# Low parts of the first expert on VectorE, its inputs in another buffer, and a later planned PE for the routing chain

## The chip, the cores and the metric

The program runs on 1 core of one Trainium2 chip. The metric is device time in microseconds (us) of one execution; lower is better. PE is TensorE, DVE is VectorE, ACT is ScalarE, POOL is GpSimd, SP is SyncE, which here only issues DMAs.

## The reference

Three layers follow one another on 4 sequences of 576 tokens: an attention with 8 heads that keeps only scores within `tau` of each row's maximum, a mixture of 8 experts (512 to 1024 to 512) with one expert per token, and a gated MLP.

```python
scores = scale * np.matmul(q, k.transpose(0, 1, 3, 2))
thresh = np.max(scores, axis=-1, keepdims=True) - tau
scores = np.where(scores >= thresh, scores, -1e9)
x = softmax(scores) @ v                       # then (B, S, 512)
...
logits = x @ w_gate; local_gate = sigmoid(x @ w_local)
for b, s:                                     # routing runs along the tokens
    fresh_e = argmax(logits[b, s])
    e = fresh_e if s == 0 or local_gate[b, s] < 0.5 else prev_e
    prev_e = e
    out[b, s] = softmax(logits[b, s])[e] * (np.maximum(x[b, s] @ w1[e], 0) @ w2[e])
...
h = gelu(x @ w_in); u, v = halves of h
out = x + (u * (w_sg @ layernorm(v) + b_sg)) @ w_out
```

Since a token's expert can be that of the token before, the routing is a chain of small dependent steps.

## The kernel before

**Order.** The kernel first makes a list of operations with their dependences, a guessed duration and a due time (`Op`, `Graph`, `Flow`). `Graph.order` plays a list scheduler over it once, when the program is built, and the instructions are written in the order that it finds. On the chip each engine runs its own queue strictly in that order: an instruction that waits holds up everything behind it on its engine. An operation marked `fill` may be put by the planner into a gap in front of a later one.

**Matmuls in two parts.** Every fp32 operand is used as a rounded high part and a low part (the rest), and a product takes three matmuls: high by high, high by low, low by high. For a weight chunk of 128 x 1024, `split` in `Tail.moe` makes the high part on ACT (`whi`) and the low part on DVE or POOL (`wlo`: raw chunk minus high part). Which engine takes it is written in a string with a letter per chunk, `WLO` for experts two to eight and `WLOA` for the first.

**The stages around the change.** The attention works on 144 tiles, whose softmax steps are on DVE (`mx`, L442, and `mask`, L466), POOL (`nb`, L452) and ACT (`ex`, L457). Each half of the tokens has a routing chain (`Route.half`): some 40 small operations, nearly all on DVE, with transposes and small matmuls on PE (L1063, L1067, L1070, L1077, L1078, and L1134 at the end, which gives the row numbers of the tokens). The first half's chain runs amid the attention. It names the expert with the most tokens, whose weights are loaded early (4 chunks of w1, 4 of w2), and picks two tiles of 128 tokens (`plain`). These two tiles need only the first half, so they are the work that PE has while the second half's chain runs: A1 is their first layer (96 matmuls of 128 x 256 columns, `fill`), A2 the second (48 matmuls of 128 x 512). `first` makes high and low part of A1's result (`hh` on ACT, `hl` on DVE). After the second half's chain POOL gathers three more tiles of the same expert (`xin`), and PE goes on with them at `L1`. `Route.rest` follows on DVE: it orders the other experts and gives the rows of the other tiles.

**Names.** Nearly all operations of the experts show line L193, that of a helper. In rows `c` (c_75 to c_80) are raw weight chunks or the attention's cells, `MR` and `r` the areas that hold rounded parts, `MF` the rest of the memory, `inv` the gathers' row numbers. The memory is cut into cells (`Mem.CELLS`); a cell that the attention has used is taken anew for rounded parts only when all of the attention's work in it is done. `RAW` are the attention's two raw buffers, at 20480 and 22528; `TURN` is the order in which the twelve weight slots are used, a slot being 2048 words at 2048 times its number; slots 0 to 3 lie in `MR`, slots 4 to 9 in the cell at 8192.

Of the kernel before, what the change touches and what calls it, by code (L numbers as in the profile page):

```python
# [8 lines left out]
F32 = mybir.dt.float32  # L9
# [5 lines left out]
AX = mybir.AxisListType  # L15
# [4 lines left out]
T = B * S  # L20
# [2 lines left out]


class Op:
    __slots__ = ("eng", "dur", "deps", "emit", "prio", "start", "end", "n", "name", "need", "cls", "users", "banks", "fill")

    def __init__(self, eng, dur, prio, emit, name):
        self.eng, self.dur, self.prio, self.emit, self.name = eng, dur, prio, emit, name
        self.need, self.cls, self.users, self.banks, self.fill = 0, None, [], None, False  # L30


class Graph:
# [4 lines left out]
        PE=dict(PE=0.0, DVE=0.2, ACT=0.2, POOL=0.27, DQ=1.29),  # L38
        DVE=dict(PE=0.256, DVE=0.12, ACT=0.135, POOL=0.156, DQ=1.22),
        ACT=dict(PE=0.227, DVE=0.145, ACT=0.1, POOL=0.17, DQ=1.245),  # L40
        POOL=dict(PE=0.161, DVE=0.075, ACT=0.12, POOL=0.1, DQ=1.17),
# [18 lines left out]
    def order(self, alpha=1.0, smax=3):  # L60
        ops = self.ops
        users = [[] for _ in ops]
        need = [0] * len(ops)
# [18 lines left out]
        def enter(o):  # L82
            t = 0.0
            for d in o.deps:
                t = max(t, d.end + self.lat(d, o.eng))
            at[o.n] = t
            ready.setdefault(o.eng, []).append(o)

# [11 lines left out]
        for o in ops:  # L100
            if not need[o.n]:
                enter(o)
        left = len(ops)
        while left:
            best = None
            for e, lst in ready.items():
# [9 lines left out]
                if c is not None and cs > f + self.GAP:  # L116
                    b = None
                    for o in lst:
                        if o.fill:
                            s = when(o, f)  # L120
                            if s + o.dur <= cs + self.GAP and (b is None or (s + alpha * o.prio, o.n) < (b[0], b[2].n)):
                                b = (s + alpha * o.prio, s, o)
# [4 lines left out]
            s, e, o = best  # L127
# [3 lines left out]
            if o.need:  # L131

                if o.need == 2:
                    b = max((b for b in (0, 2, 4, 6) if max(bank[b], bank[b + 1]) <= s), key=lambda b: max(bank[b], bank[b + 1]))
# [7 lines left out]
            for h in hold.get(o.n, ()):  # L142
                left_users[h.n] -= 1
                if not left_users[h.n]:
                    t = max(x.end + self.lat(x, "PE") for x in h.users)
# [661 lines left out]
def act(n, ps=False):  # L807
    return (0.05 if ps else 0.093) + n / 1200.0


def dve(n, two=False):
    return 0.069 + n / (1920.0 if two else 960.0)
# [6 lines left out]
def pe(n, k=1):  # L819
    return k * max(n / 2400.0 + 0.014, 0.12)  # L820


class Use:


    __slots__ = ("prev", "w", "r", "i")
# [17 lines left out]
class Bank:  # L844
    __slots__ = ("first", "w", "ap")
# [76 lines left out]
def route_consts(tc, cst):  # L922

    nc = tc.nc
    v = nc.vector
    at = [Route.CONST]

# [61 lines left out]
class Route:  # L989
# [5 lines left out]

    AT, AB, AO, SIZE = Mem.F + 8368, Mem.F + 4424, Mem.F + 5448, 3290
    CONST = AT + SIZE

    def __init__(self, g, tc, cst, prio):
        self.g, self.nc, self.cst, self.prio = g, tc.nc, cst, prio  # L1000
# [29 lines left out]

    def op(self, eng, n, emit, *deps, pr=None, pw=None, w=(), late=0.0):
        dur = n if eng in ("PE", "DQ") else dve(n) if eng == "DVE" else act(n)
        return self.g.op(eng, dur, self.p + late, emit, deps=deps, pr=pr, pw=pw, w=w, name="rt")

    def half(self, h, deps):

# [280 lines left out]
class Tail:  # L1317
# [5 lines left out]
    P = dict(more=-12.300, wld=19.348, whi=-5.770, wlo=11.562, gth=36.897, cv=31.147, xT=12.357, s=25.298, mgth=16.824, sgl=-12.676, fin=9.956, vh=63.991, sg=25.660, wo=50.081)  # L1323
    WLO = "DDDDDDDD"

    WLOA = "DDPPPPDP"
    PH = 4.0

    WR = tuple(33792 + 1024 * i for i in range(6))
    F = Mem.F  # L1330
    TURN = (0, 1, 2, 4, 6, 7, 8, 9, 5, 3, 10, 11)
    XG = (F + 6920, F + 6344, F, F + 512, F + 1024)
    XT, HH, HL, YO, G, IDX = 24576, 27648, 30720, (F + 1736, F + 2248, F + 2888), F + 4936, F + 6856
    AX, AH = 6144, (20480, 22528)
    CVA, CVF, CVC = F + 3400, (F + 8368, F + 8880, F + 9392, F + 9904), F + 10416

    def __init__(self, tc, g, cst, w1, w2, route):
# [12 lines left out]
    def slot(self, n):  # L1350
        s = self.TURN[n]
        return self.M(2048 * s, [128, 1024], F32R), self.M(2048 * s + 1024, [128, 1024], F32R)
# [15 lines left out]
    def moe(self, dep, x_dram, ys, side, sw):  # L1368

        nc, g = self.nc, self.g  # L1370
# [6 lines left out]
            wr=Ring(g, [[(a, 1024)] for a in self.WR]),  # L1377
            wh=Ring(g, [[(2048 * i, 1024)] for i in self.TURN]),
            wl=Ring(g, [[(2048 * i + 1024, 1024)] for i in self.TURN]),
            xg=Ring(g, p512(self.XG)),  # L1380
            yo=Ring(g, p512(self.YO)),
        )
        W = lambda t: self.W0 + self.ALPHA[0] * t
# [84 lines left out]
        def plain(T):  # L1468
# [10 lines left out]
            w = [ld(i, T + 1.7 * i) for i in range(4)]  # L1479
            W8 = [split(*w[i], V(T), self.WLOA[i]) for i in range(4)]  # L1480
            w += [ld(i, T + 5) for i in range(4, 8)]
            W8 += [split(*w[i], V(T + 3 + 1.3 * (i - 4)), self.WLOA[i]) for i in range(4, 8)]
            hh, hl = (self.M(a, [128, 8, z], F32R) for a in self.AH)
            hu = [g.use(*[(a + z * m, z) for a in self.AH]) for m in range(8)]
            for m in range(8):
                p = Bank()
                s = slice(m * 128, (m + 1) * 128)
                for c in range(4):
# [7 lines left out]
                    T += pe(z, 3)  # L1496
                first(m, p, hh, hl, z, hu[m], V(T) - self.PH, V(T) - self.PH)
            for t in range(NA):
# [11 lines left out]
        T, W8 = plain(0.0)  # L1510
        switch(*Mem.CELLS[3])
        base, free = NA, []
        for k, cap in enumerate(CAPS):
# [4 lines left out]
            pitch = 128 * len(tiles)  # L1518
            z = SLOTS[k] - (128 * NA if k == 0 else 0)
# [6 lines left out]
            if k:  # L1526
                st = {}
                W8 = []
                for i in range(8):
                    need = W(T + 0.3 * i if i < 4 else T + L1 + 1.3 * (i - 4))  # L1530
                    W8.append(split(*load(i, k, need, st, [dep["rank"], self.hold0]), need, self.WLO[i]))
            hh, hl = self.M(self.HH, [128, 8, pitch], F32R), self.M(self.HL, [128, 8, pitch], F32R)
            hu = [g.use((self.HH + pitch * m, pitch), (self.HL + pitch * m, pitch)) for m in range(8)]
            if k == 0:

                for x in (hh, hl):
                    g.op("POOL", 0.6, W(T - 10), lambda x=x, a=z, b=pitch: nc.gpsimd.memset(x[:, :, a:b].bitcast(F32), 0.0), w=hu, name="half")
            free = []
            for m in range(8):
                p = Bank()  # L1540
# [14 lines left out]
            for i, t in enumerate(tiles):  # L1555
                c = slice(i * 128, (i + 1) * 128)
                T = second(t, hh[:, :, c], hl[:, :, c], W8, hu, T, [R["last"]] if t == NT - 1 else ())
# [6 lines left out]
        p, o = Bank(), last  # L1564
# [6 lines left out]
        for _ in range(5):  # L1571
            o = g.op("PE", 0.645, W(T + 6), idle, deps=[o], pw=p, name="idle")
# [558 lines left out]
```

## Time and profile before

| | |
|---|---|
| median of 3 runs | 786.31 us (784.88 to 786.63) |
| the profiled execution | 785.32 us, of which the span from the first to the last instruction is 783.5 us |
| granted TensorE clock, mean over the span | 0.995 |
| PE busy | 754.4 us, 96% |
| DVE busy | 590.1 us, 75% |
| ACT busy | 456.6 us, 58% |
| POOL busy | 284.4 us, 36% |

An engine is busy while an instruction of its own runs; the shares are of the span. PE is the busiest, so its idle stretches, and the stretches in which its clock is granted at half, are where the time can change. A row of the timeline ends with the idle time before it and the instruction that ended this.

### The profile page before, as it was taken

Reading aid. Unit: us, or ns where it says so; the run is one execution under the profiler, and the core shown is the slowest. Engines: PE = TensorE matmul, PEld = TensorE weight load, DVE = VectorE, ACT = ScalarE, POOL = GpSimd, SP = SyncE. Lnnn points to the kernel's source line nnn. Section 1 sums busy time; section 2 is a strip of 40 time slices with the busy share of each in tenths; the row PEclk is TensorE's granted clock in tenths of the full one; section 3 lists DMA queues with packets and bytes.
Section 4 is the critical chain, followed back from the end, with each engine's and each line's share of the span. In section 5 each row is a group of like instructions: output and inputs, shape, how many; then the busy total and the mean of one; then the engine's idle time right before and its main releaser. Section 6 shows DMA issues by size and latency. Waiting matters only on the chain.

```text
span 783.5 us, 14050 instructions
## 1 busy us (share of the span) xinstructions
PE 754.4 (96%) x4916; PEld 652.5 (83%) x4916; DVE 590.1 (75%) x1241; ACT 456.6 (58%) x841; POOL 284.4 (36%) x435
## 2 busy tenths in 40 slices
PE   8999999999999896999999999999999999999997
PEld 5787887888787775899898998889788988888996
DVE  7999999999889979575886768794479733677632
ACT  6888888788888583163435436534486522456410
POOL 6434253433443335132533222333483333310420
PEclk9999999999999998999999999999999999999999
DMA  7342324553241441697567586733620022200012
GB/s 217 127 126 61 125 82 134 173 164 126 62 131 55 162 142 63 201 309 257 202 228 244 177 279 234 258 127 135 212 82 0 1 68 85 78 14 0 15 40 68
DMA packets 46911, 103.14 MB, mean 132 GB/s; under 512 B 7540, under 2 KB 7540, under 8 KB 46836
## 3 DMA queue, kind: packets, MB, share of 16 engines
q1 hardware_dynamic: 43636, 91.72, 35.1%
q0 software_dynamic: 3200, 10.49, 4.5%
q8 instruction: 39, 0.64, 0.3%
q14 instruction: 36, 0.29, 0.1%
HBM read 80.17 MB, written 22.02 MB: 130 GB/s over the span
## 4 chain that ended last, share of the span: by engine, by line
PE 76%; DVE 10%; ACT 8%; issue 3%; DMA 1%; POOL 1%; SPq 0%; POOLq 0%; DVEq 0%; ACTq 0%
PE PS L193 51%; PE PS L437 8%; PE PS L525 7%; PE PS L486 5%; ACT MF L457 2%; PE PS L527 2%; PE PS L540 2%; DVE MF L193 2%; DVE r L193 2%; DVE MF L442 2%; ACT c L379 1%; DVE MF L466 1%; ACT MF L193 1%; ACT MR L390 1%; POOL rq L193 1%
## 5 line engine op out<-in xcount | busy, mean ns | idle before, releaser
L193 PE MATMUL PS<-r,r 128*128 128x512 f32 (+5 forms) x1572 | 315.4, 352 | 3.4 <-DVE r L193 3.0
L193 PEld LDWEIGHTS PS<-r,r 128*128 128x128 f32 x1572 | 265.2, 188 | 36.4 <-DVE r L193 4.5
L437 PE MATMUL PS<-MR 128*128 128x288 f32 x640 | 123.4, 322 | 6.5 <-DVE MF L466 4.4
L466 DVE SCALAR_TENSOR_TENSOR MF<-PS,MF 128x576 f32<-128x576 f32 x144 | 116.0, 811 | 7.9 <-ACT MF L457 6.1
L457 ACT ACTIVATE MF<-PS,MF 128x576 f32<-128x576 f32 x144 | 106.7, 751 | 16.1 <-DVE MF L442 9.2
L442 DVE TENSOR_REDUCE MF<-PS 128x1 f32<-128x576 f32 x144 | 106.1, 751 | 4.9 <-PE PS L437 3.6
L193 PE MATMUL PS<-MR,r 128*128 128x256 f32 (+2 forms) x628 | 105.2, 322 | 0.5 <-DVE r L193 0.5
L437 PEld LDWEIGHTS PS<-MR 128*128 128x128 f32 x640 | 93.3, 192 | 14.8 <-DVE MF L466 7.9
L193 PEld LDWEIGHTS PS<-MR,r 128*128 128x128 f32 x628 | 93.8, 190 | 8.7 <-DVE r L193 0.9
L193 ACT ACTIVATE r<-PS 128x512 fp32r<-128x512 f32 (+7 forms) x110 | 47.9, 451 | 86.4 <-PE PS L193 83.8
L379 ACT ACTIVATE c<-PS 128x512 f32<-128x512 f32 (+1 forms) x160 | 85.9, 564 | 17.9 <-PE PS L486 16.8
L486 PE MATMUL PS<-ident,MF 128*128 128x128 f32 x576 | 84.9, 274 | 1.2 <-DVE c L556 0.5
L193 ACT ACTIVATE MF<-PS 128x512 f32<-128x512 f32 (+1 forms) x64 | 35.6, 558 | 79.0 <-PE PS L193 67.8
L452 POOL TENSOR_TENSOR MF<-MF,cf 128x1 f32<-128x1 f32 x120 | 28.3, 237 | 137.8 <-DVE MF L442 124.7
L486 PEld LDWEIGHTS PS<-ident,MF 128*128 128x128 f32 x576 | 67.9, 140 | 4.8 <-ACT c L379 2.1
L193 DVE SCALAR_TENSOR_TENSOR MF<-MF,PS 128x384 f32<-128x384 f32 (+1 forms) x84 | 49.9, 606 | 22.7 <-ACT MF L193 21.9
L193 DVE TENSOR_TENSOR r<-c,r 128x1024 fp32r<-128x1024 f32 x41 | 54.2, 1336 | 15.3 <-ACT r L193 14.7
L193 DVE SCALAR_TENSOR_TENSOR r<-PS,r 128x352 fp32r<-128x352 f32 (+4 forms) x72 | 30.7, 432 | 38.2 <-ACT r L193 37.8
L193 POOL TENSOR_SCALAR MF<-MF 128x512 f32<-128x512 int32 x12 | 20.5, 1704 | 95.1 <-DVE MF L193 58.1
L193 ACT ACTIVATE r<-c 128x1024 fp32r<-128x1024 f32 x47 | 48.4, 1054 | 5.9 <-PE PS L193 4.6
L193 PE MATMUL PS<-r,MR 128*128 128x352 f32 (+3 forms) x288 | 46.0, 295 | 1.7 <-DVE r L193 1.3
L193 ACT ACTIVATE r<-MF 128x256 fp32r<-128x256 f32 (+1 forms) x48 | 15.7, 358 | 53.7 <-DVE MF L193 53.5
(241 smaller groups left out, 1066.6 us busy)
## 6 DMA issues: line engine op xcount, KB each, us to landing
c<-in_w_dram SPq DMA_DIRECT2D x64, 512.0 KB, 5.3
c<-in_kP_dram SPq DMA_DIRECT2D x32, 288.0 KB, 2.9
c<-in_qP_dram SPq DMA_DIRECT2D x32, 288.0 KB, 3.0
ys<-MF SPq DMA_DIRECT2D x36, 256.0 KB, 3.9
x_dram<-c SPq DMA_DIRECT2D x6, 768.0 KB, 4.4
MF<-in_w_in_dram SPq DMA_DIRECT2D x8, 512.0 KB, 4.8
c<-in_vP_dram SPq DMA_DIRECT2D x12, 320.0 KB, 4.9
out_dram<-MF SPq DMA_DIRECT2D x12, 256.0 KB, 2.0
```

The costliest lines, as they stand in the source:

```text
L193: return lambda *a, **k: x(*[v(y) for y in a], **{n: v(y) for n, y in k.items()})
L379: self.nc.scalar.activation(out, src, AF.Copy, **k)
L390: self.nc.scalar.activation(out, src, AF.Copy, scale=f)
L437: self.nc.tensor.matmul(self.PS[:, banks[hf], 0:288], q, k[:, 288 * hf:288 * hf + 288], start=(n == 0), stop=(n == len(ops) - 1))
L442: self.nc.vector.tensor_reduce(m, self.tl[i]["s"], axis=AX.XY, op=ALU.min)
L452: (self.nc.vector if eng == "DVE" else self.nc.gpsimd).tensor_tensor(self.nbt(i), self.tl[i]["m"], self.tp, op=ALU.add)
L457: self.nc.scalar.activation(e.rearrange("p (a b) -> p a b", a=2), t["s"], AF.Exp, bias=t["m"], scale=-1.0)
L466: self.nc.vector.scalar_tensor_tensor(w.rearrange("p (a b) -> p a b", a=2), t["s"], self.nbt(i), t["e"].rearrange("p (a b) -> p a b", a=2) ...
L486: self.nc.tensor.transpose(p[:, c, :], t["w"][:, z + c * 128:z + (c + 1) * 128], self.cst["ident"])
L525: self.nc.tensor.matmul(av[r], v, self.wt(j, b)[:, c, cols], start=(c == 0), stop=False)
L527: self.nc.tensor.matmul(av, self.v4(P)[:, b, :], self.wr(P)[:, x0:x0 + 288], start=False, stop=True)
L540: self.nc.tensor.matmul(r[:, c, :], self.x2T()[:, t * 128:(t + 1) * 128], self.R[:, P % (H // 2), :])
```

## The change

- `WLOA`: the first expert's eight low parts are all made on DVE. Before, chunks 3, 4, 5, 6 and 8 of them were made on POOL.
- `AX`, `AH` and `TURN`: the two tiles' input parts stand in the attention's first raw buffer (20480) and no longer in weight slot 3 (6144). The high part of A1's result is in the second raw buffer, its low part in slot 5. The first expert's first four chunks now take slots 0 to 3, all in `MR`; the fourth was in slot 4 before.
- `PH`: the due time of `hh` and `hl` is no longer put 4 units ahead.
- `PZ`: the two POOL fills that clear the padding of the three tiles' results have a due time 60 units after L1 and no longer 10 ahead of it.
- `LAG`: for the routing chain's steps on PE the planner takes the operands to be there 0.3 us later than by its own costs.

```diff
 class Op:
-    __slots__ = (..., "users", "banks", "fill")
+    __slots__ = (..., "users", "banks", "fill", "lag")
...
     def __init__(self, eng, dur, prio, emit, name):
...
-        self.need, self.cls, self.users, self.banks, self.fill = 0, None, [], None, False
+        self.need, self.cls, self.users, self.banks, self.fill, self.lag = 0, None, [], None, False, 0.0
...
         def enter(o):
             t = 0.0
             for d in o.deps:
-                t = max(t, d.end + self.lat(d, o.eng))
+                t = max(t, d.end + self.lat(d, o.eng) + o.lag)
...
 class Route:
+    LAG = 0.3
...
     def op(self, eng, n, emit, *deps, pr=None, pw=None, w=(), late=0.0):
-        return self.g.op(eng, dur, self.p + late, emit, deps=deps, pr=pr, pw=pw, w=w, name="rt")
+        o = self.g.op(eng, dur, self.p + late, emit, deps=deps, pr=pr, pw=pw, w=w, name="rt")
+        o.lag = self.LAG if eng == "PE" else 0.0
+        return o
...
 class Tail:
-    WLOA = "DDPPPPDP"
-    PH = 4.0
+    WLOA = "DDDDDDDD"
+    PH = 0.0
+    PZ = 60
...
-    TURN = (0, 1, 2, 4, 6, 7, 8, 9, 5, 3, 10, 11)
+    TURN = (0, 1, 2, 3, 6, 7, 8, 9, 4, 5, 10, 11)
...
-    AX, AH = 6144, (20480, 22528)
+    AX, AH = 20480, (22528, 10240)
...
                 for x in (hh, hl):
-                    g.op("POOL", 0.6, W(T - 10), lambda x=x, a=z, b=pitch: nc.gpsimd.memset(x[:, :, a:b].bitcast(F32), 0.0), w=hu, name="half")
+                    g.op("POOL", 0.6, W(T + self.PZ), lambda x=x, a=z, b=pitch: nc.gpsimd.memset(x[:, :, a:b].bitcast(F32), 0.0), w=hu, name="half")
```

Line numbers of the changed kernel are 3 higher in `Route.half` (L1063 is L1066 there).

On DVE, between the end of the attention and the start of the second half's chain, before. L556 scales the attention's last results, L573 sums the logits, L1052 to L1059 are the chain's first steps, and `MR<-PS` are the low parts of the two tiles' inputs:

```order
L573 TENSOR_REDUCE MF<-c_80 128x27
L193 TENSOR_TENSOR MR<-PS,MR 128x4x128 x2
L556 TENSOR_TENSOR c_74<-PS,MF 128x3x128
L556 TENSOR_TENSOR c_80<-PS,MF 128x3x18
L573 TENSOR_REDUCE MF<-c_80 128x27
L1052 SCALAR_TENSOR_TENSOR MF<-MF 128x9
```

The same place now:

```order
L573 TENSOR_REDUCE MF<-c_80 128x27
L193 TENSOR_TENSOR r_2737<-PS,r_2737 128x4x128 x2
L193 TENSOR_TENSOR MR<-c_77,MR 128x1024
L193 TENSOR_TENSOR MR<-c_78,MR 128x1024
L193 TENSOR_TENSOR r_3112<-c_79,r_3112 128x1024
L556 TENSOR_TENSOR c_74<-PS,MF 128x3x128
L556 TENSOR_TENSOR c_80<-PS,MF 128x3x18
L193 TENSOR_TENSOR r_3112<-c_75,r_3112 128x1024
L573 TENSOR_REDUCE MF<-c_80 128x27
L1055 SCALAR_TENSOR_TENSOR MF<-MF 128x9
```

Two low parts (c_77, c_78) stand ahead of the last L556, a third (c_79) there too, and a fourth (c_75) ahead of the last L573. Of the other two that are left, one (c_76) follows behind the chain's step L1062, where before the low part from c_75 stood, and the last (c_80) stands between L1084 and L1085, where before none did. Between L1069 and L1074 four `hl` stand where there were two.

On PE, from the attention's last matmul (L527) to the chain's third step, before. The 128x256 rows are A1:

```order
L527 MATMUL PS<-c_74,c_73 128x288
L193 MATMUL PS<-MR 128x256 x6
L540 MATMUL PS<-MF 128x146 x3
L193 MATMUL PS<-MR 128x256 x21
L1063 MATMUL PS<-ident,MF 9x128
L193 MATMUL PS<-MR,r_3111 128x256 x9
L193 MATMUL PS<-MR 128x256 x3
L1067 MATMUL PS<-ident,MF 9x9
L193 MATMUL PS<-MR 128x256 x6
L1070 MATMUL PS<-ident,MF 128x9
```

The same place now:

```order
L527 MATMUL PS<-c_74,c_73 128x288
L193 MATMUL PS<-r_2737,MR 128x256 x6
L540 MATMUL PS<-MF 128x146 x3
L193 MATMUL PS<-r_2737,MR 128x256 x48
L1066 MATMUL PS<-ident,MF 9x128
L193 MATMUL PS<-r_2737,MR 128x256 x12
L1070 MATMUL PS<-ident,MF 9x9
L193 MATMUL PS<-r_2737,MR 128x256 x9
L1073 MATMUL PS<-ident,MF 128x9
```

54 of the 96 matmuls of A1 now stand ahead of the chain's first transpose, where 27 did. Further on, all 96 of A1 and 3 of A2 stand ahead of the first 18 matmuls that give the three tiles' rows (L1134), and 9 of A2 ahead of the second 18; before, 60 and 72 of A1 and none of A2 did.

On POOL, from the attention's last step (L548) to the three tiles' gathers, before:

```order
L548 TENSOR_SCALAR MF<-MF 128x6
L193 TENSOR_TENSOR MR<-c_77,MR 128x1024
L193 TENSOR_TENSOR r_3111<-c_78,r_3111 128x1024
L193 TENSOR_TENSOR r_3111<-c_79,r_3111 128x1024
L193 TENSOR_TENSOR r_3111<-c_76,r_3111 128x1024
L193 TENSOR_TENSOR r_3111<-c_80,r_3111 128x1024
L193 MEMSET r_3178 128x8x112 x2
L193 DMA MF<-x_dram,inv_91 128x512 x3
```

And now:

```order
L548 TENSOR_SCALAR MF<-MF 128x6
L193 MEMSET r_3193 128x8x112 x2
L193 DMA MF<-x_dram,inv_91 128x512 x3
```

The five low parts are gone. The two fills have stayed ahead of the three gathers.

## Rows read from the trace of the kernel before

**Rows 1.** The page's busy line: time, share of the span, instructions.

```profile
PE 754.4 (96%) x4916; PEld 652.5 (83%) x4916; DVE 590.1 (75%) x1241; ACT 456.6 (58%) x841; POOL 284.4 (36%) x435
```

**Rows 2.** Windows: PE, PEld, DVE, ACT, POOL busy, PE clock, DMA share, GB/s.

```profile
291.60:311.00 19.40, 11.74 (x111) 10.75 (x109) 17.97 (x48) 8.41 (x18) 11.56 (x7) 0.91 0.21 68
340.00:500.00 160.00, 159.54 (x921) 143.22 (x920) 116.95 (x176) 77.38 (x117) 53.18 (x39) 1.00 0.70 237
312.00:314.00 2.00, 2.00 (x11) 2.00 (x10) 1.86 (x10) 0.18 (x1) 1.50 (x2) 0.50 0.30 90
```

**Rows 3.** Timeline of PE: start, us, instructions, idle before and releaser.

```profile
291.59 2.77 PE L193 MATMUL PS<-MR 128*128 128x256 f32 x21
...
297.48 0.38 PE L1063 MATMUL PS<-ident,MF 128*9 128x128 f32 x1 [3.12 <-DVE MF L1059]
297.52 2.27 PE L193 MATMUL PS<-MR,r 128*128 128x256 f32 x9
...
300.88 0.17 PE L1067 MATMUL PS<-ident,MF 9*9 9x9 f32 x1 [0.45 <-DVE MF L1066]
...
310.40 0.61 PE L1134 MATMUL PS<-MF 128*128 128x3 bf16 x18 [4.09 <-ACT MF L1116]
310.88 2.27 PE L193 MATMUL PS<-MR 128*128 128x256 f32 x9
...
326.81 3.00 PE L193 MATMUL PS<-r,r 128*128 128x512 f32 x12
329.65 1.29 PE L193 MATMUL PS<-r,MR 128*128 128x272 f32 x9
```

**Rows 4.** Timeline of DVE, the chain's stretch, and one step of the first half's.

```profile
244.81 0.16 DVE L1054 TENSOR_TENSOR MF<-MF 128x9 f32<-128x9 f32 x1
...
291.96 0.68 DVE L556 TENSOR_TENSOR c<-PS,MF 128x384 f32<-128x384 f32 x2 [2.83 <-PE PS L540]
...
293.29 0.96 DVE L1052 SCALAR_TENSOR_TENSOR MF<-MF 128x9 f32<-128x9 f32 x1
...
294.31 2.24 DVE L1054 TENSOR_TENSOR MF<-MF 128x9 f32<-128x9 f32 x1
...
297.34 1.22 DVE L193 TENSOR_TENSOR r<-c,r 128x1024 fp32r<-128x1024 f32 x1
...
298.79 2.03 DVE L1066 TENSOR_SCALAR MF<-MF 9x9 f32<-9x9 f32 x1
...
304.26 3.83 DVE L1090 TENSOR_SCALAR MF<-MF 128x9 int32<-128x9 int32 x1
306.44 1.66 DVE L1091 TENSOR_SCALAR MF<-MF 128x9 int32<-128x9 int32 x1
...
313.29 1.74 DVE L193 SCALAR_TENSOR_TENSOR r<-PS,r 128x256 fp32r<-128x256 f32 x5
...
321.56 1.41 DVE L193 TENSOR_TENSOR r<-PS,r 128x512 fp32r<-128x512 f32 x3
```

**Rows 5.** Timeline of POOL, the chain's stretch.

```profile
291.81 4.71 POOL L193 TENSOR_TENSOR r<-c,r 128x1024 fp32r<-128x1024 f32 x2
298.01 2.79 POOL L193 TENSOR_TENSOR r<-c,r 128x1024 fp32r<-128x1024 f32 x1 [1.49 <-ACT r L193]
304.11 2.39 POOL L193 TENSOR_TENSOR r<-c,r 128x1024 fp32r<-128x1024 f32 x1 [3.31 <-ACT r L193]
306.44 1.63 POOL L193 MEMSET r<- 128x896 f32 x2
311.49 1.06 POOL L193 DMA_INDIRECT MF<-x_dram,inv  x1 [3.42 <-DVE MF L1216]
```

**Rows 6.** Timeline of ACT: three high parts of weight chunks.

```profile
290.68 2.95 ACT L193 ACTIVATE r<-c 128x1024 fp32r<-128x1024 f32 x3
```

**Rows 7.** DMA issues, 255 to 320 us (median us to landing), and all weight loads' landing.

```profile
MF<-x_dram,inv POOLq DMA_INDIRECT x5, 4.4
...
DMA to landing us min/median/max: 3.5/4.5/9.0
```

More of the change, by code (lines that the diff above doesn't have):

```diff
@@ L25 @@
 class Op:
-    __slots__ = ("eng", "dur", "deps", "emit", "prio", "start", "end", "n", "name", "need", "cls", "users", "banks", "fill")
+    __slots__ = ("eng", "dur", "deps", "emit", "prio", "start", "end", "n", "name", "need", "cls", "users", "banks", "fill", "lag")
     def __init__(self, eng, dur, prio, emit, name):
         self.eng, self.dur, self.prio, self.emit, self.name = eng, dur, prio, emit, name
-        self.need, self.cls, self.users, self.banks, self.fill = 0, None, [], None, False
+        self.need, self.cls, self.users, self.banks, self.fill, self.lag = 0, None, [], None, False, 0.0
 class Graph:
```

## The prediction

> **What bounds the kernel now.** I read the page's busy line first: PE is busy for 754.4 us of a 783.5 us span, 96%, and no other engine is near it [rows 1]. So the question is where PE stands still, and the windows by stage answer it. From 340 to 500 us PE is busy for 159.54 of 160 us; between 291.6 and 311 us, right behind the attention, it is busy for 11.74 of 19.4 us at a mean clock of 0.91 [rows 2]. The timeline of PE says what it waits for there. It is idle for 3.12 us in front of L1063, for 0.45 us in front of L1067 and for 4.09 us in front of the second L1134, 7.66 us together, and each time the releaser is a step of the second half's routing chain [rows 3]. Behind the two long waits PE runs at half clock (1.2 GHz): nine matmuls of 128x256 take 2.27 us there, while 21 take 2.77 us at full clock (2.4 GHz), 0.132 us each, so nine should take 1.19 us [rows 3]. That is 1.08 us twice, and since the window from 312 to 314 us still has the clock at 0.50 [rows 2], the second stretch goes on for 0.85 us behind its row's end, another 0.43 us. In all PE loses 7.66 + 2.59 = 10.25 us between 291.59 us and 329.65 us, where the three gathered tiles' first layer (L1) starts [rows 3]. This is also about the most that the change can give there, since it takes no matmul away.
>
> Why the chain is late stands in the timelines of DVE and POOL side by side. L1054 on 9 columns takes 0.16 us in the first half's chain and 2.24 us in the second's [rows 4]. It ends at 296.55 us, POOL's two low parts at 296.52 us; L1066 ends at 300.82 us, POOL's next low part at 300.80 us; L1090 and L1091 end at 308.1 us, POOL's two fills at 308.07 us [rows 4, 5]. So these steps waited until POOL's instruction was over. At 0.16 us for an undisturbed one, the chain lost 0.80 us at L1052, 2.08 us at L1054, 1.87 us at L1066 and 3.52 us at L1090 and L1091 (304.26 to 308.10 less two steps), 8.27 us in all.
>
> The Trainium skill has a rule for it (SBUF — State Buffer, section "Who interferes with whom"): VectorE and GpSimd share one port pair, whoever starts first holds it for a whole instruction, and a VectorE instruction with two SBUF inputs clashes only with a GpSimd instruction that reads SBUF, while a tensor_scalar in its two-port mode clashes with any. The ends above agree with it to 0.03 us. By it the five low parts are the cause, and the fills alone can still hold a tensor_scalar; that comes back as a rival.
>
> **The change, part by part.** *Low parts.* POOL's five instructions go, and with them all of the stalls but what lies behind 306.50 us, where the last of them ends [rows 5]: 6.7 us, and 8.27 us if no fill meets the chain. DVE gets five low parts at 1.22 us, the price of the one that it makes there now [rows 4]. By the built order two of them (c_77, c_78) stand in front of the last L556, where DVE is idle for 2.83 us [rows 4]: 2.44 us, hidden. The third (c_79) needs its high part, the first of three that ACT makes from 290.68 us, 0.98 us each [rows 6]: it can start at 291.7 and ends at 293.0 us, so L556, at 291.96 us before, comes 1.05 us later. The fourth (c_75) is in front of L573: 1.22 us. One (c_76) takes the place of the low part that stands behind L1059 today: nothing. The last (c_80) stands between two steps of the chain: 1.22 us. Two `hl` more stand in the chain, 0.35 us each by five in 1.74 us [rows 4]: 0.70 us. Added: 4.2 us, against 8.27 us: the chain would be 4.1 us earlier at its end.
>
> *Order on PE.* With inputs and all four first chunks in cells that are free before the attention ends, and the chain's steps planned later, 48 matmuls stand between the attention's last block and the chain's first transpose. They last from 291.6 to 291.6 + 48 x 0.132 = 297.9 us, while DVE has the operand at 297.43 - 2.88 (two stalls) + 2.27 (two low parts) = 296.8 us: PE holds the chain up by some 1.0 us, and by 0.2 us more with the 12 matmuls in front of the next transpose, since the `hl` beside it fill most of that time. So I take 2.9 us for the chain, with 4.1 us (none of it lost) and 1.3 us (a fill of 1.63 us [rows 5] falls on it too) as bounds. The second L1134 then starts at 310.40 - 2.9 = 307.5 us.
>
> PE gets there with 90 matmuls of A1 (11.9 us), nine of A2 at 0.237 us (12 in the 2.84 us from 326.81 to 329.65 us [rows 3]; 2.1 us), one L1134 block (0.61 us) and some 0.6 us of transposes, at 306.8 us: 0.7 us of idle time is left of the 4.09, and the 3.12 are gone. I take it that the clock stays full, since 0.45 us of idle time did not bring it down and only 3.12 and 4.09 us did; a drop again would cost up to 1.5 us.
>
> *Behind it.* From 310.40 to 329.65 us there are 19.25 us now. Of them go 24 matmuls of A1 (3.2 us), the half clock (1.5 us) and nine of A2 (2.1 us), which come earlier: 12.45 us, so L1 at 319.95 us. What is late next is the gathers. The first is issued 1.09 us behind the L1134 block [rows 3, 5], so at 308.6 us, the second 1.37 us later, and they land 4.4 us after issue in the median [rows 7]: the second at 314.4 us. PE is at its transposes after 21 more matmuls of A2 and the first tile's, at 313.7 us: 0.7 us of new waiting. On DVE the steps of `rest` end 11.16 us after the second L1134 now (321.56 us [rows 4]), 0.70 us less with two `hl` gone ahead: 318.0 us, and the three low parts behind them 1.41 us more, 319.4 us, still ahead of PE. So L1 starts at 320.65 us, 9.0 us earlier; by the other way, 10.25 us lost now less 0.7 and 0.7, it is 8.85 us. I take 8.9 us.
>
> *The rest.* The fills have not moved behind the three gathers in POOL's queue, only ahead in time, as the five low parts are gone. The later planned steps of the first half's chain and the first high part, which ACT now makes amid the attention, move things by tenths there; I take 0 with 1.0 us either way. The second expert's loads come behind a store of A2's result on SP, so they move up less than PE does; I take it that the chunks wait long enough for this not to matter.
>
> Since PE has no slack behind L1 [rows 2], the 8.9 us go through to the end: the profiled execution of 785.32 us becomes 776.4 us. The median of the runs is 0.99 us above the profiled one (786.31 us), so I predict 777.4 us.
>
> **The rivals.** A change under 0.2%, 1.6 us, is about what a measurement of this kernel can't tell from none.
>
> *The chain is no earlier.* If PE's order and DVE's added work eat all of the 4.1 us, the second L1134 stays at 310.40 us; L1 still starts 12.45 + 0.7 us behind it, at 323.55 us, since A1 is done by then. That is 6.1 us of gain, 780.2 us, and 4.6 us or 781.7 us if the longer idle time takes the clock down again. For it: five instructions more on DVE, which is busy for 17.97 of 19.4 us there [rows 2]; against it: nearly half of these busy 17.97 us are the stalls.
>
> *The fills fall on the chain.* They run as soon as their cell is free, which no row of before times, but now ahead of the end of the chain's first steps. If L1066's successor, a tensor_scalar, meets them, it waits for up to 1.63 us [rows 5]; with 1.1 us in the shadow of PE's 12 matmuls the price is 0.5 us, else 1.6 us: 779.0 us. By the Trainium skill's rule above they can meet only that kind of step.
>
> *Given back at the later experts.* If the weights' loads and not PE set the pace from the second expert on, then only what the loads move up is kept. They wait for the gathers' landing, some 2.5 us earlier: 783.8 us. Against it: DMA engines are busy at 0.70 while PE is full [rows 2].
>
> *Slower.* The first high part stands amid the softmax steps on ACT now and waits there for its load. Weight loads land 3.5 to 9.0 us after issue [rows 7]. If this one were at the slow end, ACT and behind it the attention would stand for some 5 us, leaving 782.4 us; it decides only from about 9 us of standing on, and 2 us beyond it would be 788.4 us.
>
> **How the numbers follow.** My forecast, 7 to 10.5 us of gain with the fills' half microsecond in it, gets 0.56; the chain no earlier 0.18; the fills at full price 0.08; given back 0.10; slower, by ACT's wait or something that I don't see, 0.08. The range is 774.0 to 783.0 us: its lower end is all of the 10.25 us, the attention's 1.0 us and a little for PE's small steps, its upper end lies just under the case that gives the gain back. Faster by over 0.2%: 0.87, with the first three and half of the fourth counted wholly; same 0.05; slower 0.08.
>
> **What would show it.** In the changed kernel's trace L1057 and L1069 (L1054 and L1066 before) should take some 0.2 us, PE's idle time between the attention's end and L1 should be under 2 us, with no window at clock 0.50, the second L1137 should start near 307.5 us and L1 near 320.7 us, if the attention ends where it did. I am wrong if the chain's steps stay long with POOL idle, if DVE's L556 starts well behind 293.0 us, or if PE shows new gaps behind 340 us that add up to microseconds.

## The result, and the profile after

| | before | changed |
|---|---|---|
| median of four runs, us | 786.14 | 776.95 |
| lowest to highest, us | 784.88 to 786.63 | 775.96 to 777.45 |
| profiled execution, us (span) | 785.32 (783.5) | 777.45 (775.5) |

The ratio is 0.9884 with a 95% interval of 0.9867 to 0.9901: the changed kernel is 9.2 us faster. The forecast was 777.4 us.

The page of the changed kernel, its span and busy line, to be read beside [rows 1]:

```profile
span 775.5 us, 14046 instructions
PE 751.9 (97%) x4916; PEld 649.6 (84%) x4916; DVE 587.2 (76%) x1246; ACT 456.3 (59%) x841; POOL 272.0 (35%) x430
```

The windows, whose last three columns are the clock, the DMA share and GB/s, to be read beside [rows 2]:

```profile
291.60:311.00 19.40, 19.05 (x161) 16.99 (x160) 17.66 (x75) 8.46 (x19) 3.92 (x5) 1.00 0.25 82
...
506.00:508.00 2.00, 2.00 (x12) 2.00 (x11) 1.26 (x3) 0.33 (x1) 0.00 (x0) 0.50 0.35 131
```

Behind the attention PE is busy for 19.05 of 19.4 us, where it was busy for 11.74, and at full clock. But there is a stretch at half clock from 505 us on that the kernel before does not have. The timeline of PE, behind the attention and near 505 us:

```profile
291.66 5.94 PE L193 MATMUL PS<-r,MR 128*128 128x256 f32 x48
297.44 0.27 PE L1066 MATMUL PS<-ident,MF 128*9 128x128 f32 x1
...
299.23 0.17 PE L1070 MATMUL PS<-ident,MF 9*9 9x9 f32 x1
...
306.54 0.61 PE L1137 MATMUL PS<-MF 128*128 128x3 bf16 x18 [0.24 <-ACT MF L1119]
...
312.89 0.66 PE L193 MATMUL PS<-ident,MF 128*128 128x128 f32 x4 [0.42 <-DMA MF<-x_dram,inv]
...
314.72 0.66 PE L193 MATMUL PS<-ident,MF 128*128 128x128 f32 x4 [0.48 <-DMA MF<-x_dram,inv]
...
319.81 1.66 PE L193 MATMUL PS<-r,MR 128*128 128x272 f32 x12
321.32 0.61 PE L1261 MATMUL PS<-MF 128*128 128x14 bf16 x18
...
323.37 0.61 PE L1261 MATMUL PS<-MF 128*128 128x14 bf16 x18
...
502.26 1.58 PE L193 MATMUL PS<-r,MR 128*128 128x192 f32 x12 [0.73 <-DVE r L193]
504.48 7.24 PE L193 MATMUL PS<-r,MR 128*128 128x192 f32 x48 [0.63 <-DVE r L193]
```

Against [rows 3]: the waits of 3.12 and 4.09 us are gone, 0.24 + 0.42 + 0.48 = 1.14 us of waiting is left up to L1 (the row of 128x272), and L1 starts at 319.81 instead of 329.65 us. Two L1261 blocks stand behind its start.

The timeline of DVE in the chain and near 500 us, then POOL's, to be read beside [rows 4, 5]; the last row is ACT's first high part:

```profile
292.98 0.67 DVE L556 TENSOR_TENSOR c<-PS,MF 128x384 f32<-128x384 f32 x2
...
295.51 0.16 DVE L1057 TENSOR_TENSOR MF<-MF 128x9 f32<-128x9 f32 x1
...
298.36 0.81 DVE L1069 TENSOR_SCALAR MF<-MF 9x9 f32<-9x9 f32 x1
...
304.05 0.17 DVE L1093 TENSOR_SCALAR MF<-MF 128x9 int32<-128x9 int32 x1
...
499.65 2.29 DVE L193 TENSOR_TENSOR r<-c,r 128x1024 fp32r<-128x1024 f32 x1
...
502.13 2.03 DVE L193 TENSOR_TENSOR r<-c,r 128x1024 fp32r<-128x1024 f32 x1
...
297.52 1.64 POOL L193 MEMSET r<- 128x896 f32 x2 [11.80 <-DMA x_dram<-c]
...
499.57 3.51 POOL L193 TENSOR_TENSOR MF<-MF 128x512 f32<-128x512 f32 x2
...
267.33 1.06 ACT L193 ACTIVATE MR<-c 128x1024 fp32r<-128x1024 f32 x1 [0.83 <-DMA c<-in_w_dram]
```

L1057 takes 0.16 us instead of 2.24, L1093 0.17 instead of 3.83. Only L1069 is still held: it ends at 299.17 us and POOL's fills end at 299.16 us. And near 500 us the old pattern stands in another stage: two low parts of DVE take 2.29 and 2.03 us instead of 1.22 while POOL's conversion of a later weight chunk runs (499.57 to 503.08 us), and it is for DVE that PE waits there. By single instructions the two engines take turns: POOL's first ends at 500.86 us, DVE's first low part 1.08 us later (501.94), POOL's second 1.14 us after that (503.08, it takes 2.14 us where the first took 1.29), DVE's second 1.08 us after that (504.16). So DVE holds POOL there as POOL holds DVE. Below, "the lock" is this mutual holding.

### The profile page after: what moved, and what is told of

Same layout as the page of the kernel before. It is cut to its first block, busy times and chain, and to the rows that moved or that the text cites. A ratio compares the mean times of both kernels' runs of the same rounds, so it can differ in the third digit from the quotient of the medians.

```text
span 775.5 us, 14046 instructions
## 1 busy us (share of the span) xinstructions
PE 751.9 (97%) x4916; PEld 649.6 (84%) x4916; DVE 587.2 (76%) x1246; ACT 456.3 (59%) x841; POOL 272.0 (35%) x430
## 4 chain that ended last, share of the span: by engine, by line
PE 48%; DVE 5%; ACT 2%; DMA 1%; issue 1%; POOL 1%; POOLq 0%; ACTq 0%
PE PS L193 48%; DVE MF L193 2%; DVE r L193 2%; ACT MF L193 1%; ACT r L193 1%; POOL rq L193 0%; DVE bs L193 0%; DMA MF<-ys,MF 0%; DMA c<-ys,MF 0%; DMA out_dram<-MF 0%; DMA ys<-MF 0%; POOL MR L193 0%; DVE MR L193 0%; DVE rq L193 0%; DVE mv L193 0%
## 5 line engine op out<-in xcount | busy, mean ns | idle before, releaser
L193 PE MATMUL PS<-r,r 128*128 128x512 f32 (+4 forms) x1544 | 300.8, 351 | 3.5 <-DVE r L193 2.9
L193 PEld LDWEIGHTS PS<-r,r 128*128 128x128 f32 x1544 | 256.7, 188 | 35.0 <-DVE r L193 4.8
L437 PE MATMUL PS<-MR 128*128 128x288 f32 x640 | 121.7, 319 | 6.8 <-DVE MF L466 3.9
L193 PE MATMUL PS<-MR,r 128*128 128x256 f32 (+2 forms) x616 | 101.7, 322 | 0.1
L193 PEld LDWEIGHTS PS<-MR,r 128*128 128x128 f32 x616 | 91.5, 188 | 8.9 <-DVE r L193 0.6
L193 DVE TENSOR_TENSOR r<-c,r 128x1024 fp32r<-128x1024 f32 x44 | 56.9, 1314 | 15.7 <-ACT r L193 14.9
L193 PE MATMUL PS<-r,MR 128*128 128x256 f32 (+3 forms) x384 | 54.4, 300 | 1.8 <-DVE r L193 1.4
L193 PEld LDWEIGHTS PS<-r,MR 128*128 128x128 f32 x384 | 52.4, 195 | 2.8 <-DVE r L193 1.7
```

The lines of the kernel that those rows point to most:

```text
L193: return lambda *a, **k: x(*[v(y) for y in a], **{n: v(y) for n, y in k.items()})
L437: self.nc.tensor.matmul(self.PS[:, banks[hf], 0:288], q, k[:, 288 * hf:288 * hf + 288], start=(n == 0), stop=(n == len(ops) - 1))
```

## The experiments

All ratios are against the kernel before, run on the same chip.

**1. Five low parts back on POOL** (in the changed kernel).

```
-    WLOA = "DDDDDDDD"
+    WLOA = "DDPPPPDP"
```

> The changed kernel with five of the eight low parts back on POOL; buffers, the fills' place and the later planned chain steps stay as changed. Theory (POOL's low parts hold the chain's steps on DVE until they end): the five low parts run on POOL from the attention's end on, L1057 or L1069 take 1 to 2 us again, the chain's last step comes some 4 to 8 us later than in the changed kernel, PE stands idle for 4 to 8 us ahead of the L1137 blocks at least once with a stretch at clock 0.50 behind it, and the time is 782 to 786 us. Rival (the buffers and the order on PE bring the gain, the engine of the low parts doesn't matter): L1057 stays near 0.2 us or PE has enough matmuls left to cover the stalls; idle under 2 us; 776 to 778.5 us.

Measured: 784.21 us, ratio 0.999 (0.9973 to 1.0006). The timelines of DVE, POOL and PE:

```profile
294.11 2.25 DVE L1057 TENSOR_TENSOR MF<-MF 128x9 f32<-128x9 f32 x1
296.28 2.44 DVE L1058 TENSOR_TENSOR MF<-MF 128x72 f32<-128x72 f32 x1
...
293.97 4.66 POOL L193 TENSOR_TENSOR r<-c,r 128x1024 fp32r<-128x1024 f32 x2
...
299.51 0.28 PE L1066 MATMUL PS<-ident,MF 128*9 128x128 f32 x1 [4.88 <-DVE MF L1062]
...
311.43 0.61 PE L1137 MATMUL PS<-MF 128*128 128x3 bf16 x18 [2.44 <-ACT MF L1119]
```

The window behind the first wait, whose third column from the end is the clock:

```profile
300.00:302.00 2.00, 2.00 (x11) 1.86 (x9) 1.66 (x5) 1.03 (x4) 0.00 (x0) 0.50 0.00 0
```

L1058 ends at 298.72 us, POOL's second pair of low parts at 298.63 us. The held steps are a little longer than the theory had it, and the longest wait is in front of L1066 instead of an L1137 block; the time is as it said: the whole gain is gone with this one edit, new cells and all. The edit also changes the planner's order, since the low parts have other engines and costs: 24 matmuls of A1 stand between the attention's last block and L1066, no longer 48. So the rival, that cells and order make the gain while the low parts' engine doesn't matter, is out only together with experiment 6, which keeps the order.

**2. Low parts on DVE alone** (in the kernel before).

```
-    WLOA = "DDPPPPDP"
+    WLOA = "DDDDDDDD"
```

> The kernel before with one change, all eight low parts on DVE; old buffers, old place of the fills, no later planning. Theory (the lock is what costs, order and buffers are the smaller part): L1054 at 0.2 us, the stalls of 8.27 us gone, but 69 matmuls of A1 instead of 48 stand ahead of the chain's first transpose, so PE reaches it 21 x 0.124 = 2.6 us later than in the changed kernel; PE is idle for 2 to 3 us more than the changed kernel later on, in front of the second L1134 block; 778.5 to 781 us. Rival A (low parts on DVE are all of it): 776.5 to 778 us. Rival B (the order on PE is most of it): PE stands as long as before, 783 to 786 us.

Measured: 780.89 us, ratio 0.9937 (0.9915 to 0.996), half of the gain. The timeline of PE:

```profile
299.59 0.27 PE L1063 MATMUL PS<-ident,MF 128*9 128x128 f32 x1
...
306.65 0.60 PE L1134 MATMUL PS<-MF 128*128 128x3 bf16 x18 [0.46 <-ACT MF L1116]
...
311.74 1.08 PE L193 MATMUL PS<-ident,MF 128*128 128x128 f32 x4 [3.68 <-DMA MF<-x_dram,inv]
```

The window behind the long wait:

```profile
312.00:314.00 2.00, 2.00 (x8) 1.60 (x7) 1.79 (x13) 0.60 (x1) 0.07 (x1) 0.50 0.55 164
```

The time is within the theory's numbers, the place isn't: the second L1134 comes at 306.65 us, in the changed kernel at 306.54. The attention ends 0.41 us earlier here, so the later first transpose costs some half a microsecond. What costs more is behind it. PE has spent its matmuls ahead of the chain and has in its order only three more ahead of the tiles' transposes, stands for 3.68 us until the first tile has landed, and falls to half clock. The rest of the change is worth what it keeps for this place.

**3. Old cells; 4. no later planning; 5. the old due times of `hh`, `hl` and the fills** (each in the changed kernel).

```
-    TURN = (0, 1, 2, 3, 6, 7, 8, 9, 4, 5, 10, 11)
+    TURN = (0, 1, 2, 4, 6, 7, 8, 9, 5, 3, 10, 11)
...
-    AX, AH = 20480, (22528, 10240)
+    AX, AH = 6144, (20480, 22528)
```

> The changed kernel with the cells of the first expert's inputs and chunks, and the turn of the cells, as before. 57 matmuls of A1 stand ahead of the chain's first transpose instead of 48. Theory (the chain's first transpose is held by what PE has queued ahead of it, and a microsecond of it costs about that at the second L1137): the transpose is 9 x 0.124 = 1.1 us later, the second L1137 at 307.3 to 308 us instead of 306.5 with 0.5 to 1.5 us more of idle time; 777.5 to 779 us. Rival (the buffers are most of the gain, since inputs that come late make PE or DVE wait for loads): waits for a load of an input or chunk ahead of A1, over 3 us of idle time, 780 us or more. Second rival (buffers do nothing): within 0.6 us of the changed kernel.

```
-    LAG = 0.3
+    LAG = 0.0
```

> The changed kernel with the chain's steps on PE planned without the 0.3 us. 45 matmuls of A1 stand ahead of the first transpose instead of 48, then 12, 6 and 6 instead of the changed kernel's. Theory (what counts is that PE always has work where the chain's operand isn't there yet; the transposes come about as their operands do): PE is idle for 0.2 to 0.5 us in front of each of three or four steps of the chain, the second L1137 at 306.3 to 307.3 us, the time 776.5 to 778.5 us, within 0.2% of the changed kernel. Rival (the later planning is a main part): the transposes come ahead of their operands, over 2 us of idle time and a stretch at clock 0.50; 779 us or more.

```
-    PH = 0.0
-    PZ = 60
+    PH = 4.0
+    PZ = -10
```

> The changed kernel with the low parts' costs in the plan and the fills' due time as before; POOL's order stays the same, on DVE and PE some `hl` and matmuls shift. Theory (the fills' new due time moves nothing where it matters): within 0.8 us of the changed kernel, 776.2 to 777.8 us, L1069 held by a fill for 0.5 to 1 us as there. Rival (the fills' place is worth something): over 1.6 us slower, with a fill on L1069, L1093 or L1094 of over 1.5 us.

Measured: old cells 776.73 us, ratio 0.9884 (0.9856 to 0.9912); no later planning 778.70 us, 0.9912 (0.9883 to 0.9942); old due times 777.14 us, 0.9893 (0.9879 to 0.9907). The timeline of PE with old cells:

```profile
307.51 0.61 PE L1137 MATMUL PS<-MF 128*128 128x3 bf16 x18
```

The timeline of PE without the later planning:

```profile
304.75 0.61 PE L1137 MATMUL PS<-MF 128*128 128x3 bf16 x18 [0.40 <-ACT MF L1119]
...
309.95 0.63 PE L193 MATMUL PS<-ident,MF 128*128 128x128 f32 x4 [1.75 <-DMA MF<-x_dram,inv]
...
311.97 0.63 PE L193 MATMUL PS<-ident,MF 128*128 128x128 f32 x4 [0.70 <-DVE MF L1232]
```

The old cells make the chain 1 us later and the time no longer, so the theory missed there (777.5 us or more) and its second rival, that cells do nothing, holds. Without the later planning the chain is 1.8 us *earlier* than in the changed kernel and the time 1.75 us longer, with an interval that overlaps the changed kernel's: PE gets to the tiles early and stands for 1.75 + 0.70 + 0.43 us there (for the first of these the trace names the landing, for the other two a step of DVE). Neither forecast had that place; the theory's 776.5 to 778.5 us is missed by 0.2. The old due times move the time by no more than the runs spread, as expected, but not the trace: the second L1137 comes at 308.03 us and L1 at 321.28 us, both 1.5 us later than in the changed kernel, and L1069 takes 0.26 us, so the fills don't hold it there, against the theory.

**6. POOL writes instead of reading** (in the kernel before; the five low parts of POOL are left out of the result, and three fills of the same cell stand in the place of each).

```
-... lambda: nc.gpsimd.tensor_tensor(l, raw, h.bitcast(F32), op=ALU.subtract), ...
+... lambda: [nc.gpsimd.memset(l.bitcast(F32), 0.0) for _ in range(3)], ...
```

> The kernel before, with each of the five low parts of POOL replaced by three fills of the same cell, so that POOL is as long at work in the same places but reads nothing; it leaves these five low parts out of the result. Theory (POOL holds DVE by the port for reading, so steps of DVE with two inputs, L1052 and L1054, are held only by a POOL instruction that reads; a tensor_scalar as L1066 can be held by any): L1052 and L1054 at 0.2 us, L1066 at up to 1.1 us (the rest of one fill), L1090 and L1091 held by fills as before; the chain's first transpose is set by PE and not by DVE. Rival A (any POOL instruction holds any DVE step): L1052 or L1054 at 0.8 us or more. Rival B (the steps were not held by POOL but waited for something else that ends there): L1054 at about 2.2 us as before.

Measured: 778.37 us, one run, beside a median of 785.5 us for the kernel before. The timelines of DVE, POOL and PE:

```profile
293.55 0.16 DVE L1054 TENSOR_TENSOR MF<-MF 128x9 f32<-128x9 f32 x1
...
296.01 0.65 DVE L1066 TENSOR_SCALAR MF<-MF 9x9 f32<-9x9 f32 x1
...
298.70 0.89 DVE L1101 TENSOR_SCALAR MF<-MF 128x9 f32<-128x9 int32 x1
298.81 0.77 DVE L1080 TENSOR_TENSOR MF<-MF 128x72 f32<-128x72 bf16 x1
...
300.61 0.99 DVE L1090 TENSOR_SCALAR MF<-MF 128x9 int32<-128x9 int32 x1
...
289.85 13.36 POOL L193 MEMSET r<- 128x1024 f32 x14 [1.12 <-PE PS L525]
...
304.46 0.61 PE L1134 MATMUL PS<-MF 128*128 128x3 bf16 x18 [2.15 <-ACT MF L1116]
```

POOL is at work without a break from 289.85 to 303.21 us, longer than in the kernel before, and L1054 takes 0.16 us instead of 2.24. So POOL's being busy doesn't hold a step with two inputs: a fill, which only writes, doesn't, and a subtraction, which also reads, does. The tensor_scalar steps are held, each for under 1 us, as long as a fill lasts (13.36 / 14 = 0.95 us). Two steps with two inputs are long too, L1080 (0.77 us, 0.22 before) and L1097 (0.58, 0.19 before); each stands right behind a held tensor_scalar (L1101, L1092) and ends within 0.01 us of it. I take them to be held by the step ahead of them and not by the fill; no run tells the two apart. The Trainium skill (SBUF — State Buffer, "Who interferes with whom") says that a DVE instruction with two inputs in SBUF clashes with a GpSimd instruction that reads SBUF and not with one that only writes it, and that one in its two-port mode, which a tensor_scalar can enter, clashes with GpSimd. Both halves show here. That it is the reading, and not another difference between a subtraction and a fill, is the Trainium skill's word; no run puts another reading POOL instruction in the chain's place.

This single run also prices the holding alone, since it has the order and cells of before and no added work on DVE: L1 starts at 322.90 instead of 329.65 us, 6.75 us earlier, the half clock behind the long waits included. One expectation fails: the first transpose is still set by DVE, for which PE waits 0.29 us there.

**7. The conversion off POOL**, to see whether the lock near 500 us can be taken away too (in the changed kernel; both steps, then the sum alone, then both with the old cells of experiment 3).

```
-g.op("POOL", pool(512), T, lambda: nc.gpsimd.tensor_tensor(c, c, p.bitcast(F32), op=ALU.mult), ...
-g.op("POOL", pool(512), T, lambda: nc.gpsimd.tensor_tensor(c, c, f.bitcast(F32), op=ALU.add), ...
+g.op("DVE", 0.6, T, lambda: v.tensor_tensor(c, c, p.bitcast(F32), op=ALU.mult), ...
+g.op("DVE", 0.6, T, lambda: v.tensor_tensor(c, c, f.bitcast(F32), op=ALU.add), ...
```

> The changed kernel with the last two steps of each weight chunk's conversion (a product and a sum, 128x512) on DVE instead of POOL. Theory (near 500 us DVE's low parts take 2.0 to 2.3 us instead of 1.2 because POOL's conversion holds the shared port, PE then stands for 0.73 and 0.63 us and falls to half clock for some 3 us): the low parts take 1.2 to 1.3 us there, those two gaps are under 0.2 us, no window at clock 0.50 near 505 us; 2.5 to 3 us less than the changed kernel, 774 to 775 us. Rival A (DVE's added steps, 0.6 us or more each, come late for the low parts just as the lock did): the gaps stay, within 0.6 us of the changed kernel. Rival B (DVE, busy for 0.7 of that stretch, becomes late for the steps that free PE's banks): new gaps behind 340 us, 778 us or more.

> The changed kernel itself, to stand beside the three others on one chip. Its profiled execution shows PE at clock 0.50 for some 3.6 us from 505 us on, behind two gaps of 0.73 and 0.63 us; three experiments with the same two gaps don't show it. Theory (whether the clock falls there differs from one execution to the next): the time is 776 to 778 us either way; if the window at 506 to 508 us shows clock 1.00 the span is 1.5 to 2 us under the 775.5 us of the profile known so far. Rival (the order of this kernel brings it down each time): clock 0.50 from 506 to 508 us again.

> The same kernel as in the run with both conversion steps on DVE, again, now beside the changed kernel. Theory (POOL's conversion holds DVE's low parts as POOL's low parts held the chain): 1 to 3 us under the changed kernel on the same chip, low parts of 1.22 us near 498 us. Rival (the earlier 775.31 us against 776.95 us was spread between runs): within 1 us of the changed kernel.

> The changed kernel with only the last of the conversion's two two-input steps (the sum) on DVE, the product left on POOL. Theory: the lock lasts half as long, so one low part near 500 us is held and the other is not; between the changed kernel and the one with both steps moved, 775.5 to 777 us. Rival (each step on DVE costs what its lock cost): as the changed kernel or slower, 777 us or more.

> Both conversion steps on DVE, and the first expert's inputs and chunks in the cells of before. Alone, the cells of before gave the changed kernel's time to 0.3 us. Theory (cells don't matter, the lock does): within 1 us of the kernel with both steps on DVE, 774 to 776 us. Rival (with DVE busier the later chunks make the chain wait): 777 us or more.

Measured: both steps 775.31 us (773.59 to 778.87), ratio 0.9884 (0.9866 to 0.9902). Then on one chip: the changed kernel 776.22 us, 0.9883 (0.9864 to 0.9902); both steps again 775.36 us (773.79 to 778.12), 0.9872 (0.985 to 0.9894); the sum alone 776.18 us, 0.9885 (0.9863 to 0.9908); both with old cells 777.88 us, 0.9898 (0.9878 to 0.9919). The timelines of DVE and PE with both steps on DVE, first run:

```profile
498.64 1.22 DVE L193 TENSOR_TENSOR r<-c,r 128x1024 fp32r<-128x1024 f32 x1
...
503.62 0.43 DVE L193 TENSOR_SCALAR MF<-MF 128x512 int32<-128x512 int32 x1 [1.53 <-DMA MF<-in_w_in_dram]
...
504.69 0.35 DVE L193 SCALAR_TENSOR_TENSOR r<-PS,r 128x192 fp32r<-128x192 f32 x1
...
505.10 2.93 PE L193 MATMUL PS<-r,MR 128*128 128x192 f32 x24 [1.14 <-DVE r L193]
```

The low parts are back at 1.22 us, so POOL's two steps had held them. But PE has one wait of 1.14 us where it had 0.73 and 0.63: DVE now comes to the first step on the next chunk before that chunk has landed, waits 1.53 us for it (0.17 us in the changed kernel), and the `hl` for which PE waits stands behind it in DVE's order. One wait took another's place (1.53, 1.31 and 0.85 us on PE in the other three), and no version is faster than the changed kernel by more than the intervals leave open. So the theories of the four runs fail in part: the waits are not gone, both steps on DVE miss 774 to 775 us by 0.3 us and are 0.86 us faster than the changed kernel on the same chip where 1 to 3 us were forecast (the rival, within 1 us, holds), and with old cells the 777.88 us fall to the rival (777 us or more). Only the sum alone lies within its theory's bounds, and there it can't be told from the changed kernel.

The changed kernel again, the timeline of PE:

```profile
502.46 1.58 PE L193 MATMUL PS<-r,MR 128*128 128x192 f32 x12 [0.71 <-DVE r L193]
504.68 5.60 PE L193 MATMUL PS<-r,MR 128*128 128x192 f32 x48 [0.64 <-DVE r L193]
```

And the window behind it:

```profile
506.00:508.00 2.00, 2.00 (x21) 2.00 (x19) 1.83 (x4) 0.63 (x2) 0.00 (x0) 1.00 0.35 131
```

The same two waits, full clock, and 48 matmuls in 5.60 instead of 7.24 us: the order doesn't bring the clock down there each time. The span is 774.2 us, 1.3 us shorter: the 1.64 us, less 0.31 us by which L1 comes later in this execution (320.12 us). The clock fell in another place, though, to 0.50 from 10 to 12 us, where it costs next to nothing: the first transpose comes 0.04 us later (297.48 us). The mean granted clock is 0.997 in all nine runs of the changed kernel, so the others may each hold such a stretch; no trace shows where.

**8. Low parts on DVE and the later planning, nothing else** (the changed kernel with the edits of experiments 3 and 5 together).

> Two parts of the change alone: low parts on DVE and the later planning of the chain's steps on PE; cells, turn and the fills' due time as before. 69 matmuls of A1 stand ahead of the chain's first transpose, as in the run with the low parts alone, but more of A2 stands between the later steps. Theory (low parts give the chain its steps back, the later planning keeps PE at work until the gathers land, cells and fills only shift it by tenths): the second L1137 at 308 to 309.5 us, some 2 us later than with the low parts alone, no idle time of over 2 us behind it and no window at clock 0.50, 777 to 779 us. Rival (the cells and the fills' place are needed for the second half of the gain): an idle time of 2 us or more ahead of the first tile's transposes, with half clock behind it, 780 to 781.5 us as with the low parts alone.

Measured: ratio 0.9904 (0.987 to 0.9938), 784.26 against 790.66 us on a chip that ran both kernels some 5 us slower and less evenly. The timelines of PE and, last, ACT:

```profile
309.34 0.61 PE L1137 MATMUL PS<-MF 128*128 128x3 bf16 x18 [0.45 <-ACT MF L1119]
...
315.00 0.63 PE L193 MATMUL PS<-ident,MF 128*128 128x128 f32 x4 [0.85 <-DMA MF<-x_dram,inv]
...
553.74 4.58 PE L193 MATMUL PS<-r,r 128*128 128x512 f32 x12 [4.26 <-DVE r L193]
...
552.36 1.33 ACT L193 ACTIVATE r<-PS 128x512 fp32r<-128x512 f32 x2 [6.41 <-remote]
```

Up to L1, which starts at 321.46 us, all is as the theory said: the second L1137 within its bounds, no wait of 2 us, full clock. L1 starts can be compared once the small matmuls of L1261 (L1258 before) are counted alike: all 72 stand ahead of L1 in the kernel before and with low parts alone, 36 of them (0.93 us) behind it here and in the changed kernel. On that footing L1 comes 4.08 us earlier with low parts alone (325.57 us), 7.26 us with the two parts and 8.91 us with the whole change (319.81 us). So these two parts are most of the change, but not all of it. The median isn't to be read that finely: the interval reaches to both forecasts, and the profiled execution lost 3.3 us at 553.74 us (4.26 against 0.98 in the changed kernel), behind an ACT step whose releaser the trace gives as "remote", and some 1.6 us at half clock behind that (the 12 matmuls take 4.58 us, 3.02 in the changed kernel). What held ACT stays open.

## Why the prediction was right

**The stalls.** Right: POOL's low parts cost the chain its steps. Experiment 1 brings the stalls back, and experiment 6 takes them away with POOL still at work and the order unchanged.

**Added work on DVE.** Right: L556 was forecast at 293.0 us and starts at 292.98.

**PE holding the chain.** Right in kind, too large. The first transpose was forecast at 297.9 and came at 297.44 us: the 48 matmuls take 5.78 us up to it, 0.120 us each, not 0.132. That figure came from one row of 21 in 2.77 us. Two rows together say that each further matmul costs (5.94 - 2.77) / 27 = 0.117 us and that a row has some 0.3 us beside, which a division by 21 spreads over the matmuls. From there to the second L1137 it is 9.10 us, 0.5 us less than forecast, so that this comes at 306.54 instead of 307.5 us.

**The fills.** The rival was there: L1069 takes 0.81 us. Its price is some 0.3 us, not the forecast's 0.5 to 1.6: the 12 matmuls of A1 in front of L1070 last to 299.13 us, L1066 shows that the next one can start 0.16 us ahead of such an end (297.44 against 297.60 us), and L1070 starts at 299.23.

**Gathers.** 0.7 us of new waiting was forecast; it is 0.42 + 0.48 us, the second of them at the third tile.

**L1.** Forecast at 320.65 us, measured 319.81, but the comparison with before overlooks that all 72 L1258 matmuls stood ahead of L1 and 36 of them stand behind its start now, 0.93 us in two blocks. The gain up to there is 9.84 - 0.93 = 8.91 us; 8.9 was forecast, and that this fits so well is luck: the second L1137 came 0.96 us earlier than forecast, and the stretch from there to L1, forecast at 13.15 us, took 13.27 + 0.93 = 14.20 us. Of these 1.05 us the gathers explain 0.2; the rest isn't traced to a cause.

**The rest.** Here the step "the 8.9 us go through to the end" was mis-sized for the profiled execution: the span is 8.0 us shorter. The stretch at half clock takes 7.24 - 5.60 = 1.64 us. Against it, three waits that the kernel before has are absent: the first of these rows (timeline of PE, before), and 0.17 and 0.24 us near 690 us. The other two rows show that the two waits near 500 us are not new; the kernel before has them at full clock:

```profile
383.50 4.47 PE L193 MATMUL PS<-MR,r 128*128 128x512 f32 x18 [0.46 <-DVE r L193]
...
511.37 1.25 PE L193 MATMUL PS<-r,MR 128*128 128x192 f32 x9 [0.66 <-DVE r L193]
513.59 1.25 PE L193 MATMUL PS<-r,MR 128*128 128x192 f32 x9 [0.63 <-DVE r L193]
```

8.91 - 1.64 + 0.87 = 8.14 us; the waits that both kernels have behind L1 are 0.1 us longer together, such as 0.73 us for 0.66. The median's gain, 9.19 us, is a little over the forecast, within what the runs spread.

**The other rivals.** The chain is 3.86 us earlier, so the first is out. Behind L1 nothing was given back but the clock's 1.64 us. ACT waited 0.83 us for its load, not 5, and the attention ended 0.07 us later.

## What to carry to other kernels

When small steps of a chain end in the very moment at which another engine's instruction ends, look at what that engine's instructions do, not at how busy it is: writing alone left the two-input steps free, though not the tensor_scalar steps. In these versions, with the second L1137 between 304.75 and 308.03 us, an earlier chain was no longer a shorter time; what PE has left to do while the gathers are under way mattered more: the version with the earliest second L1137 of the changed kernel's edits (304.75 us) was no faster than the one at 307.51 us. And a wait that is taken out of an engine that works in order is only gain if the next thing in its queue is ready: in experiment 7 DVE then stood for 1.53 us in front of a chunk that had not landed.

## What the hardware showed that was not expected

Idle time of PE and the clock behind it don't go together simply. In these traces the clock was at 0.50 behind waits of 3.12 and 4.09 us [rows 2, 3], 4.88 us (experiment 1) and 3.68 us (experiment 2), and at 1.00 behind 2.44 (experiment 1), 2.15 (6) and 1.75 us (4); but behind 0.73 and 0.63 us, 2.2 us apart, it fell to 0.50 once and stayed at 1.00 in the same kernel's next profile. Near 8 us it was the other way round: at 1.00 behind 1.42 and 0.34 us in the first profile, at 0.50 behind 1.58 and 0.36 us in the next. The prediction's remark that 0.45 us of idle time had not brought it down was too little to rest a term on.
